# Preparing the fifth attention half three units later, and the second network's weight conversion nine units later, in a fused attention and two-network kernel

## The chip, the core and the metric

The kernel runs on one core of one Trainium2 chip. The metric is the device time of one execution in microseconds (us), as the median of several runs; lower is better. The core's engines are named as in the profile: PE (TensorE, matmuls), PEld (TensorE's weight loads), DVE (VectorE), ACT (ScalarE), POOL (GpSimd) and SP (SyncE, which here issues nearly all transfers).

## The reference

Three stages run one after the other. The first is a linear attention with a decaying state: 4 batches, 8 heads, 768 steps, head size 48. Its output, 3072 tokens of 384 numbers, goes through a network with a rational activation (384 to 2048 to 384), and then through a second network with a softmax-weighted activation and a normalisation (384 to 1024 to 384).

```
state = alpha[:, :, t, :, None] * state + einsum('bhd,bhe->bhde', k[:, :, t], v[:, :, t])
y[:, :, t] = einsum('bhd,bhde->bhe', q[:, :, t], state)
...
h = x @ w_in
P = a[0] + a[1]*h + a[2]*h**2 + a[3]*h**3
Q = 1.0 + abs(b[0])*abs(h) + abs(b[1])*h**2
x2 = (P / (Q + 1e-06)) @ w_out
...
h = x2 @ w_in2
solu = h * softmax(h)
out = (normalise(solu) * g_ln) @ w_out2
```

## The kernel before

**Chunks and units.** The 768 steps are cut into 6 chunks of 128 steps; with 4 batches a chunk has 512 tokens. The first network runs over one chunk after the other. A **unit** is one chunk and one block of 128 of the 2048 hidden columns, so a chunk has 16 units (`NF1`), and there are 96 (`NU`), counted by `u`. For each unit `m_up` multiplies (9 matmuls of 128x512, line 595, into the PSUM tile `hp`), ACT, DVE and POOL compute the rational activation, and `m_down` of the unit four before (`LAG = 4`) multiplies again (9 matmuls, line 641, into `x2p`). Numbers are split into a high and a low part, which is why each product takes three matmuls. Units below 24 with an even number (`MIX`) give part of the activation to POOL: DVE has three passes there, lines 613, 618 and 619; the other units have four, lines 621, 624, 625 and 626. `hp` has three buffers: the matmuls of unit u wait for the last DVE pass (line 619 or 626) of unit u-3.

**Halves.** A chunk's attention is done in two **halves** of two batches each, so there are 12, counted by `i` from 0. From `i = 2` on, a half is **prepared** by `a_dve`: transposes of alpha, k and q (lines 291 and 296), a running product (scan `P`, line 309), a reverse scan (line 318), a product (line 321), two transposes back (line 325), with POOL's product at line 336, which SP then moves through DRAM into the tiles `qks` (lines 338 and 277) and `kns` (lines 330 and 283). **Computed** it is by `a_pe`: two rounds of scores on PE (`sc`, line 421), copied by ACT (line 428) and masked by POOL (line 429), then the outputs `y` (line 445), written to the next chunk's input `xt` (lines 471 and 472), and the state update `u` (lines 486, 496 and 497).

**Order around the change.** The main loop over `u` calls `half_steps(i)` at every eighth unit, when `u` modulo 8 is `LATE = 2`: half 2 at unit 2, half 3 at unit 10, half 4 (the fifth) at unit 18, and so on. It makes one step of `a_pe(i)` and two steps of the preparation of half `i + 1` in each unit. So the fifth half is prepared in units 10 to 14, beside the computation of half 3. The helper `pin` ties those steps to work of units shortly before; within that the order on each engine is settled by the scheduler when the program is built, and is then fixed: each engine works its list in order.

**Weights.** The inputs of both networks' weights are 64-bit numbers; `split_w` brings them in (line 536), converts them on DVE (lines 540, 543 and 544), and splits them on ACT and POOL (lines 550 and 551). The first network's are converted in groups during the first chunk. The second network's are converted by `w2_split`, 14 steps (six of 512 columns, eight of 384), and stored to DRAM (line 553). One step is taken in each unit from `U2 = 15` on in which `IDLE` holds: units 15, 16, 24, 25, 32, 33 and so on to 64, 65. They are read again from unit 80 on.

Of the kernel before, what the change touches and what calls it, by code (L numbers as in the profile page):

```python
# [23 lines left out]
def _run(*gens):  # L24
    for g in gens:
        for _ in g:
            pass
# [3 lines left out]
def kernel(  # L31
# [25 lines left out]
    NF1 = DF1 // 128  # L57
# [5 lines left out]
    NPE = 2  # L63
# [12 lines left out]
    GS = 2  # L76
# [4 lines left out]
    SKIP = (5, 7, 11)  # L81
    AHEAD = 3
    HOLD = (1, NCH - 1)
    LATE = 2
    U2, IDLE = NF1 - 1, lambda u: (u + (u < NF1 + 4)) % (NF1 // 2) < 2
    assert (B, H, D, CH) == (4, 8, 48, 128)

    const = ctx.enter_context(tc.tile_pool(name="const", bufs=1, side="left"))
# [65 lines left out]
    def network(fast):  # L154
# [98 lines left out]
        def a_load(i, names=("ra", "rk", "rq")):  # L253
            for x, (src, nm) in enumerate(((alpha, "ra"), (k, "rk"), (q, "rq"))):
                if nm not in names:
                    continue
                if i == 1:
                    t = borrow(3, 2048 + 1024 * x, [16 * D + 16])
                elif i == 0 and nm == "rq":
                    t = borrow(3, 5120, [16 * D + 16])  # L260
                else:
                    t = ap_.tile([128, 16 * D + 16], F32, name=nm, tag="rk" if nm == "rk" else "ra")
                if i < NPE:
                    nc.gpsimd.memset(t[:, 16 * D:], 1.0)
                for y in range(B):
                    c, b, h = slot(i, y)
                    nc.sync.dma_start(  # L267
                        out=t[32 * y:32 * y + 32, :16 * D].rearrange("p (h x) -> p h x", h=4),
                        in_=src[b, h:h + 4, CH * c:CH * c + CH, :].rearrange("h (j r) d -> j h (r d)", r=4),
                    )  # L270
                raws[i, nm] = t
                yield

        def a_move_qk(i):
            qk, kb = moved[i]
            for m, i0, n, d0 in ((0, 0, 32, 0), (1, 0, 16, 32), (1, 16, 16, 64), (2, 0, 32, 80)):
                nc.sync.dma_start(out=qks[d0:d0 + n], in_=qk[m].rearrange("b i x -> i b x")[i0:i0 + n])
            yield
# [122 lines left out]
        def a_prep(i):  # L401
            if i >= NPE:
                yield from a_dve(i)

        def a_enter(i):
            if i < NPE:
                v_load(i)
                yield from a_turn(i)
            else:
                yield from a_move(i)  # L410

        def a_pe(i):
# [21 lines left out]
            end = ap_.tile([128, B, 2], F32, name="end", tag="end", bufs=2)  # L434
# [38 lines left out]
            yield  # L473
            if i >= NPE:
                yield
            if i >= 2 * NPE:
                yield
            if i < NPE:
                a_back(i)
            u = ps_ap.tile([128, B * 2, D], F32, name="u", tag="at")  # L480
# [185 lines left out]
        def w2_load(nm):  # L666
            src = {"i": w2i_d, "o": w2o_d}[nm]
            n, step = {"i": (KT, 1), "o": (NF2, 4)}[nm]
            for z in range(0, n, step):
                for x, y in enumerate("hl"):  # L670
                    nc.sync.dma_start(out=w2[nm + y][:, z:z + step].bitcast(F32), in_=src[:, x, z:z + step])
                    yield
# [140 lines left out]
        def chain(*gens):  # L813
            for g in gens:
                yield from g
# [34 lines left out]
        now = [0]  # L850
        NU = NCH * NF1
# [4 lines left out]
        def pin(n):  # L856
            stack = ExitStack()
            if n <= now[0] < NU and fast:
                for e, u in (("PE", now[0]), ("ACT", now[0] - n), ("POOL", now[0] - n)):
                    stack.enter_context(tc.issue_after(last[e, u].ins))  # L860
                stack.enter_context(tc.issue_after(fin[now[0] - n].ins))
            return stack

        def half_steps(i):
            gp = a_pe(i)
            gd = chain(a_prep(i + 1), a_move_qk(i + 1) if i + 1 >= NPE else iter(()), a_load(i + 2, ("ra", "rk")) if i + 2 < NH and i + 1 >= NPE else iter(())) if i + 1 < NH else iter(())
            while True:
                with pin(GP):
                    a = next(gp, "end")
                with pin(GS):  # L870
                    b = next(gd, "end")
                    if b != "end":
                        b = next(gd, "end")
                if a == "end" and b == "end":
                    if i + 1 < NH:
                        _run(a_enter(i + 1))
                        if i + 2 < NH and i + 1 < NPE:
                            _run(a_load(i + 2))
                    return
                yield  # L880
# [6 lines left out]
        for u in range(NU + LAG):  # L887
            c, f = divmod(u, NF1)
            now[0] = u
            if f % (NF1 // 2) == LATE and u < NU:  # L890
                _run(side)
                i = 2 * c + 2 + f // (NF1 // 2)
                side = half_steps(i) if fast and i < NH else iter(())
            if u < NU:
                if f == 0 and c == NCH - 1:
                    if fast:
                        judge(moe_pool)
                    open2()
                    tail = chain(w2_load("i"), n_load(0), w2_load("o"))
                if f == 0 and c and not fast:  # L900
                    x_load(c)
                if fast and u < NF1:
                    if f % 4 == 0:
                        _run(prep)
                        if f:
                            stage["near"] = False
                            stage["bank"] = ""
                        prep = w1_group(f // 4 + 2) if f < 8 else iter(())
                    with later(G1):
                        take(prep, 1)  # L910
                m_up(u)
                if fast and u < NF1:
                    with later(G1):
                        take(prep, 1)
            if u == NU:
                _run(n_load(1))
            take(side, 1)
            if u >= U2 and IDLE(u):
                stage["bank"] = "at"
                with later(G2):  # L920
                    take(split2, 1)
            if tail is not None:
                _run(split2)
                take(tail, 2)
            if u >= LAG:
                held.append(u - LAG)
            if not (f == LAG and HOLD[0] < c < HOLD[1]):
                while held:
                    m_down(held.pop(0))
            if u - NU + NF1 in EARLY:  # L930
                n_tile(EARLY.index(u - NU + NF1))
                if len(EARLY) == B and u - NU + NF1 == EARLY[-1]:
                    n_turn(0)
        ps_h.__exit__(None, None, None)
        ps_x2.__exit__(None, None, None)
        end = ExitStack()
# [106 lines left out]
    with tc.If(wide > 0):  # L1043
        recurrence()
        network(False)
# [30 lines left out]
```

## Time and profile before

| | us |
|---|---|
| median of 3 runs | 771.57 |
| lowest and highest | 770.66, 771.99 |
| the profiled execution | 771.29 |
| its span, first to last instruction | 769.4 |
| busy in the span: PE | 727.3 |
| DVE | 625.1 |
| ACT | 535.2 |
| POOL | 359.2 |

The profiled execution's time is 1.89 us above its span. Busy times are sums over the whole span; the stages have different limits, so the stretches around units 10 to 20 have to be read by themselves. In the trace unit 10's first matmuls start at 120.44 us and unit 20's at 177.09 us.

### The profile page before, as it was taken

How to read it: one execution, taken by the hardware profiler on the slowest of the kernel's cores; microseconds unless marked ns; L12 is line 12 of the kernel's file. 1: busy time of each engine (PE TensorE's matmuls, PEld its weight loads, DVE VectorE, ACT ScalarE, POOL GpSimd, SP SyncE). 2: the span in 40 equal slices, each digit the busy share in tenths (PEclk: the TensorE clock that was granted, in tenths of full speed). 3: DMA queues.
4: the chain of work that ended last, by engine and by line, in shares of the span. 5: the costliest groups of instructions: out<-in, count | busy, mean ns of one | idle time of the engine just before them, and what ended most of it. 6: DMA issues, size and time to landing. Idle time of an engine off the chain costs nothing.

```text
span 769.4 us, 13908 instructions
## 1 busy us (share of the span) xinstructions
PE 727.3 (95%) x4976; PEld 605.7 (79%) x4976; DVE 625.1 (81%) x1111; ACT 535.2 (70%) x984; POOL 359.2 (47%) x306
## 2 busy tenths in 40 slices
PE   4686999999999999999999999999999999999996
PEld 3575767788888888778787788888888989988996
DVE  5999999989899989898998966567787797877630
ACT  2245867688878878797979788888965565555641
POOL 3255787877555345444445523422243333442322
PEclk9857899999999999999999999999999999999998
DMA  7994447475747483726554350820025354451552
GB/s 174 264 278 153 106 149 173 127 171 174 165 153 182 136 182 95 186 79 193 133 146 89 117 91 1 302 109 0 2 83 126 96 123 117 114 123 43 138 130 67
DMA packets 87278, 101.74 MB, mean 132 GB/s; under 512 B 34464, under 2 KB 63136, under 8 KB 87200
## 3 DMA queue, kind: packets, MB, share of 16 engines
q1 hardware_dynamic: 87008, 100.41, 49.2%
q8 instruction: 41, 0.67, 0.4%
q10 hardware_dynamic: 192, 0.36, 0.2%
q14 instruction: 37, 0.30, 0.1%
HBM read 60.59 MB, written 27.56 MB: 115 GB/s over the span
## 4 chain that ended last, share of the span: by engine, by line
PE 58%; DVE 24%; issue 5%; DMA 5%; ACT 4%; SPq 2%; POOL 0%; DVEq 0%; ACTq 0%; POOLq 0%
PE hp L595 14%; PE x2p L641 13%; PE op L787 13%; PE h L716 13%; DVE w L624 3%; DVE hp L625 2%; DVE p L626 2%; DVE p L621 2%; SPq L267 2%; PE y L445 2%; DMA rq<-in_q_dram 1%; DVE qk L291 1%; DVE ft L544 1%; DVE alT L325 1%; DVE fp L543 1%
## 5 line engine op out<-in xcount | busy, mean ns | idle before, releaser
L595 PE MATMUL hp<-xt,g 128*128 128x512 f32 x864 | 222.8, 401 | 15.6 <-DVE p L619 7.5
L629 POOL TENSOR_TENSOR gl<-p,gh 128x512 fp32r<-128x512 f32 x96 | 134.6, 1402 | 206.0 <-ACT gh L628 117.7
L595 PEld LDWEIGHTS hp<-xt,g 128*128 128x128 f32 x864 | 163.1, 192 | 57.3 <-DVE p L626 11.2
L641 PE MATMUL x2p<-gh,g 128*128 128x512 f32 x576 | 195.5, 395 | 0.4 <-ACT gh L628 0.4
L641 PEld LDWEIGHTS x2p<-gh,g 128*128 128x128 f32 x576 | 107.7, 188 | 26.3 <-ACT gh L628 1.6
L641 PE MATMUL x2p<-gl,g 128*128 128x512 f32 x288 | 113.0, 392 | 0.0
L787 PE MATMUL op<-w2oh,room 128*128 128x384 f32 x384 | 101.5, 338 | 0.0
L779 POOL TENSOR_TENSOR room<-room,room 128x1024 fp32r<-128x1024 f32 x22 | 53.8, 2448 | 101.7 <-ACT room L778 81.0
L624 DVE SCALAR_TENSOR_TENSOR w<-w,co,hp 128x512 f32<-128x512 f32 x84 | 62.0, 738 | 45.4 <-ACT hp L623 44.5
L716 PE MATMUL h<-w2ih,x 128*128 128x512 f32 x288 | 90.8, 394 | 0.0
L602 ACT ACTIVATE p<-hp,co 128x512 f32<-128x512 f32 x96 | 66.1, 688 | 13.7 <-POOL gl L629 13.0
L603 ACT ACTIVATE w<-ah,co 128x512 f32<-128x512 f32 x96 | 69.4, 724 | 6.9 <-DVE hp L625 6.7
L787 PEld LDWEIGHTS op<-w2oh,room 128*128 128x128 f32 x384 | 70.1, 188 | 0.9
L600 ACT ACTIVATE ah<-hp 128x512 f32<-128x512 f32 x96 | 57.0, 593 | 16.2 <-PE hp L595 15.6
L621 DVE SCALAR_TENSOR_TENSOR p<-p,co,hp 128x512 f32<-128x512 f32 x84 | 61.8, 736 | 7.6 <-ACT p L602 7.3
L623 ACT ACTIVATE hp<-ah 128x512 f32<-128x512 f32 x84 | 50.2, 598 | 25.3 <-DVE p L621 24.3
L787 PE MATMUL op<-w2ol,room 128*128 128x384 f32 x192 | 65.0, 339 | 0.0
L628 ACT ACTIVATE gh<-p 128x512 fp32r<-128x512 f32 x96 | 59.9, 624 | 6.6 <-PE x2p L641 3.4
L641 PEld LDWEIGHTS x2p<-gl,g 128*128 128x128 f32 x288 | 54.1, 188 | 11.7 <-issue 0.8
L626 DVE SCALAR_TENSOR_TENSOR p<-p,co,hp 128x512 f32<-128x512 f32 x84 | 62.4, 742 | 1.0
L716 PEld LDWEIGHTS h<-w2ih,x 128*128 128x128 f32 x288 | 53.9, 188 | 11.7
L622 ACT ACTIVATE ah<-w,co 128x512 f32<-128x512 f32 x84 | 60.8, 724 | 1.1
(168 smaller groups left out, 1258.6 us busy)
## 6 DMA issues: line engine op xcount, KB each, us to landing
room<-room SPq DMA_DIRECT2D x94, 128.0 KB, 2.4
qk_d<-qk SPq DMA_DIRECT2D x10, 771.0 KB, 4.1
st<-in_moe_w_in_dram SPq DMA_DIRECT2D x13, 512.0 KB, 4.6
st<-in_moe_w_out_dram SPq DMA_DIRECT2D x16, 384.0 KB, 3.2
qks<-qk_d SPq DMA_DIRECT2D x20, 257.0 KB, 4.3
x<-x_d SPq DMA_DIRECT2D x18, 256.0 KB, 3.1
out_dram<-o SPq DMA_DIRECT2D x94, 48.0 KB, 1.6
ra<-in_alpha_dram SPq DMA_DIRECT2D x44, 96.0 KB, 2.4
```

What stands on the lines that cost most here:

```text
L595: last["PE", u] = nc.tensor.matmul(hp, lhsT=w[:, kt, 128 * o:128 * o + 128], rhs=xts[c][:, kt, xx, :], start=(kt == 0 and w is hi and xx = ...
L602: nc.scalar.activation(p, hp, AF.Square, bias=co[:, 7:8])
L603: nc.scalar.activation(w, ah, AF.Square, bias=co[:, 6:7])
L621: nc.vector.scalar_tensor_tensor(p, p, a1, hp, ALU.add, ALU.mult)
L622: nc.scalar.activation(ah, w, AF.Ln, bias=rest)
L624: nc.vector.scalar_tensor_tensor(w, w, rest, hp, ALU.add, ALU.mult)
L626: fin[u] = nc.vector.scalar_tensor_tensor(p, p, a0, hp, ALU.add, ALU.mult)
L628: last["ACT", u] = nc.scalar.activation(gh, p, AF.Copy)
L629: last["POOL", u] = nc.gpsimd.tensor_tensor(gl, p, gh[:].bitcast(F32), ALU.subtract)
L641: nc.tensor.matmul(x2ps[c][d], lhsT=w[:, o, 128 * d:128 * d + 128], rhs=gg, start=(f == 0 and w is hi and gg is gh), stop=(f == NF1 - 1 an ...
L716: nc.tensor.matmul(hp[:, 512 * n:512 * n + 512], lhsT=x2s[c][:, kt, x, CH * b:CH * b + CH], rhs=w2[w][:, kt, 512 * n:512 * n + 512], start ...
L787: nc.tensor.matmul(op, lhsT=x[:, 128 * f:128 * f + 128], rhs=w2[w][:, f, :], start=(f == 0 and x is hi and w == "oh"), stop=(f == NF2 - 1 ...
```

## The change

Three edits to when things are issued; no computation is added or taken away.

- The preparation of the fifth half (issued beside half 3) begins at unit 13 instead of 10, by `WAIT = {3: 13}`. At two steps a unit it now takes units 13 to 17.
- `half_steps(4)`, with the fifth half's scores and the preparation of the sixth, begins at unit 19 instead of 18. One empty step of `a_pe` is left out for this half, so its state update stays at unit 23 and the halves after it stay where they were.
- `w2_split` begins at unit 24 instead of 15: units 24, 25, 32, 33 and so on to 72, 73.

```
-    LATE = 2
-    U2, IDLE = NF1 - 1, lambda u: (u + (u < NF1 + 4)) % (NF1 // 2) < 2
+    LATE = lambda u: u % (NF1 // 2) == (3 if u // (NF1 // 2) == 2 else 2)
+    WAIT = {3: 13}
+    U2, IDLE = NF1 + 4, lambda u: u % (NF1 // 2) < 2
...
-            if i >= 2 * NPE:
+            if i > 2 * NPE:
                 yield
...
-                with pin(GS):
-                    b = next(gd, "end")
-                    if b != "end":
+                b = None
+                if now[0] >= WAIT.get(i, 0):
+                    with pin(GS):
                         b = next(gd, "end")
+                        if b != "end":
+                            b = next(gd, "end")
...
-            if f % (NF1 // 2) == LATE and u < NU:
+            if LATE(u) and u < NU:
```

Line numbers of the functions above are one higher in the changed kernel. The lists of the engines are the same in both kernels up to unit 9's first DVE pass; there they part.

On DVE, between unit 9's first pass (line 621) and its last (line 626), the list before holds the fifth half's transposes of alpha and its scan:

```order
L543 SCALAR_TENSOR_TENSOR ft<-st,ft 128x384
L296 STREAM_TRANSPOSE alT<-ra 128x4x32
L624 SCALAR_TENSOR_TENSOR w<-w,co,hp 128x512
L544 SCALAR_TENSOR_TENSOR ft<-st,ft 128x384
L309 SCALAR_TENSOR_TENSOR P<-alT,d_109 128x774
L613 SCALAR_TENSOR_TENSOR hp<-p,co,hp 128x512
L540 TENSOR_SCALAR ft<-st 128x384
L625 SCALAR_TENSOR_TENSOR hp<-w,hp 128x512
L496 TENSOR_TENSOR Sbd<-Sbd,u 48x8x48 x2
L618 SCALAR_TENSOR_TENSOR hp<-hp,co,ah 128x512
L543 SCALAR_TENSOR_TENSOR ft<-st,ft 128x384
L626 SCALAR_TENSOR_TENSOR p<-p,co,hp 128x512
```

and of the change the same stretch, up to unit 9's last pass (now line 627):

```order
L544 SCALAR_TENSOR_TENSOR ft<-st,ft 128x384
L545 SCALAR_TENSOR_TENSOR ft<-st,ft 128x384
L625 SCALAR_TENSOR_TENSOR w<-w,co,hp 128x512
L614 SCALAR_TENSOR_TENSOR hp<-p,co,hp 128x512
L541 TENSOR_SCALAR ft<-st 128x384
L626 SCALAR_TENSOR_TENSOR hp<-w,hp 128x512
L497 TENSOR_TENSOR Sbd<-Sbd,u 48x8x48 x2
L544 SCALAR_TENSOR_TENSOR ft<-st,ft 128x384
L541 TENSOR_SCALAR ft<-st 128x384
L627 SCALAR_TENSOR_TENSOR p<-p,co,hp 128x512
```

The transposes and the scan are gone from it, and one more conversion piece of the first network's weights (a second line 541) stands ahead of the last pass.

Still on DVE, from unit 13's last pass to the state update of half 3 (`Sbd`), the list before holds the first two conversion steps of the second network's weights (`fp`):

```order
L626 SCALAR_TENSOR_TENSOR p<-p,co,hp 128x512
L472 TENSOR_TENSOR xt<-y,xt 128x2x256
L472 TENSOR_TENSOR xt<-y,xt 128x256
L540 TENSOR_SCALAR fp<-st 128x512
L543 SCALAR_TENSOR_TENSOR fp<-st,fp 128x512
L613 SCALAR_TENSOR_TENSOR hp<-p,co,hp 128x512
L544 SCALAR_TENSOR_TENSOR ft<-st,fp 128x512
L540 TENSOR_SCALAR fp<-st 128x512
L543 SCALAR_TENSOR_TENSOR fp<-st,fp 128x512
L618 SCALAR_TENSOR_TENSOR hp<-hp,co,ah 128x512
L544 SCALAR_TENSOR_TENSOR ft<-st,fp 128x512
L496 TENSOR_TENSOR Sbd<-Sbd,u 48x8x48 x2
```

and of the change, with the second part of the fifth half's preparation there:

```order
L627 SCALAR_TENSOR_TENSOR p<-p,co,hp 128x512
L292 STREAM_TRANSPOSE qk<-rq 128x2x4x32
L614 SCALAR_TENSOR_TENSOR hp<-p,co,hp 128x512
L326 STREAM_TRANSPOSE alT<-qk 128x3x4x32 x2
L297 STREAM_TRANSPOSE qk<-rq 128x4x32 x2
L619 SCALAR_TENSOR_TENSOR hp<-hp,co,ah 128x512
L292 STREAM_TRANSPOSE qk<-rq 128x2x4x32
L620 SCALAR_TENSOR_TENSOR p<-w,hp 128x512
L622 SCALAR_TENSOR_TENSOR p<-p,co,hp 128x512
L497 TENSOR_TENSOR Sbd<-Sbd,u 48x8x48 x2
```

The conversion has left this place. The preparation's first part now stands between unit 11's last pass and unit 13's last.

On SP, before, the transfers of the fifth half stand behind two loads of the second network's weights (line 536), and two stores of them (line 553) stand behind:

```order
L536 DMA st<-in_moe_w_in_dram 128x512 x2
L330 DMA kb_d<-alT 128x768
L267 DMA ra<-in_alpha_dram 32x4x192 x4
L338 DMA qk_d<-qk 128x3x514
L277 DMA qks<-qk_d 32x4x514
L277 DMA qks<-qk_d 16x4x514 x2
L277 DMA qks<-qk_d 32x4x514
L349 DMA vns<-in_v_dram 128x8x48 x2
L283 DMA kns<-kb_d 128x4x192
L553 DMA w2i_d<-st 256x1x512 x2
```

and of the change:

```order
L331 DMA kb_d<-alT 128x768
L350 DMA vns<-in_v_dram 128x8x48
L268 DMA ra<-in_alpha_dram 32x4x192 x4
L350 DMA vns<-in_v_dram 128x8x48
L284 DMA kns<-kb_d 128x4x192
L339 DMA qk_d<-qk 128x3x514
L278 DMA qks<-qk_d 32x4x514
L278 DMA qks<-qk_d 16x4x514 x2
L278 DMA qks<-qk_d 32x4x514
```

The loads and stores of weights have left, and `vns` and `kns` now stand ahead of the move of `qks`.

## Rows read from the trace of the kernel before

**Rows 1.** Windows by engine: length, then busy us (instructions), clock, DMA share, GB/s.

```profile
118.00:151.00 33.00, 30.46 (x266) 24.08 (x264) 32.77 (x56) 23.27 (x43) 26.40 (x23) 1.00 0.57 147
151.00:300.00 149.00, 149.00 (x1135) 121.30 (x1134) 135.53 (x222) 127.17 (x230) 83.27 (x76) 1.00 0.63 161
440.00:480.00 40.00, 40.00 (x322) 32.63 (x321) 27.09 (x40) 33.75 (x60) 14.13 (x14) 1.00 0.30 60
```

**Rows 2.** Timeline of PE, 130 to 150 us: start, length, instruction, idle before.

```profile
131.77 2.16 PE L421 MATMUL sc<-qks 48*128 48x128 f32 x16
135.16 2.34 PE L595 MATMUL hp<-xt,g 128*128 128x512 f32 x9 [1.23 <-DVE p L626]
...
142.15 0.41 PE L445 MATMUL y<-A,vns 128*32 128x128 f32 x4 [0.74 <-POOL A L429]
...
148.00 0.73 PE L595 MATMUL hp<-xt,g 128*128 128x512 f32 x2 [0.57 <-DVE p L626]
```

**Rows 3.** Windows on DVE, instructions of tile alT alone: length, busy (instructions).

```profile
123.80:134.30 10.50, 3.66 (x5) 1.00 0.75 180
134.30:147.20 12.90, 4.66 (x4) 1.00 0.39 121
```

**Rows 4.** The same of tile qk alone, the whole preparation.

```profile
123.80:149.20 25.40, 6.47 (x13) 0.38 (x2) 0.00 (x0) 1.00 0.55 151
```

**Rows 5.** Groups of DVE, 123.8 to 149.2 us, by shape: busy, mean ns, idle before.

```profile
L325 DVE STREAM_TRANSPOSE alT<-qk 128x384 f32<-128x384 f32 x2 | 1.6, 855 | 0.0
...
L321 DVE TENSOR_TENSOR qk<-qk,alT 128x768 f32<-128x768 f32 x1 | 0.9, 945 | 0.0
```

**Rows 6.** Timeline of DVE: last passes of units 9, 11 and 14.

```profile
134.37 0.73 DVE L626 SCALAR_TENSOR_TENSOR p<-p,co,hp 128x512 f32<-128x512 f32 x1
...
147.24 0.71 DVE L626 SCALAR_TENSOR_TENSOR p<-p,co,hp 128x512 f32<-128x512 f32 x1
...
160.78 0.68 DVE L619 SCALAR_TENSOR_TENSOR p<-w,hp 128x512 f32<-128x512 f32 x1
```

**Rows 7.** Timeline of POOL: state products, two masks of scores, the preparation's product.

```profile
134.01 2.03 POOL L497 TENSOR_TENSOR Sbd<-Sbd,end 48x384 f32<-48x384 f32 x2
...
139.99 2.10 POOL L429 TENSOR_SCALAR_AFFINE_SELECT A<-A 128x512 f32<-128x512 f32 x1
...
146.92 0.64 POOL L429 TENSOR_SCALAR_AFFINE_SELECT A<-A 128x512 f32<-128x512 f32 x1
...
149.26 1.74 POOL L336 TENSOR_TENSOR qk<-qk,P 128x768 f32<-128x768 f32 x1 [0.44 <-DVE qk L291]
```

**Rows 8.** Groups of DVE, 153 to 159.1 us: the second network's first two conversions.

```profile
L543 DVE SCALAR_TENSOR_TENSOR fp<-st,fp 128x512 int32<-128x512 int32 x2 | 1.4, 698 | 0.1
L540 DVE TENSOR_SCALAR fp<-st 128x512 int32<-128x512 int32 x2 | 1.4, 696 | 0.1
L544 DVE SCALAR_TENSOR_TENSOR ft<-st,fp 128x512 int32<-128x512 int32 x2 | 1.4, 680 | 0.0
```

**Rows 9.** Timeline of PE around units 17 to 19.

```profile
164.21 4.24 PE L595 MATMUL hp<-xt,g 128*128 128x512 f32 x18
...
169.75 1.16 PE L421 MATMUL sc<-qks 48*128 48x128 f32 x16
...
173.01 2.20 PE L595 MATMUL hp<-xt,g 128*128 128x512 f32 x9
```

**Rows 10.** Timeline of SP's queue: the move of the fifth half's qks.

```profile
152.46 0.39 SPq L338 DMA_DIRECT2D qk_d<-qk  x1
156.56 1.73 SPq L277 DMA_DIRECT2D qks<-qk_d  x4
```

**Rows 11.** Transfers of tile qks, 140 to 240 us: time from issue to landing.

```profile
DMA to landing us min/median/max: 3.3/4.4/5.7
```

**Rows 12.** Timeline of PE: idle behind the conversions of units 48 and 56.

```profile
328.91 2.34 PE L595 MATMUL hp<-xt,g 128*128 128x512 f32 x9 [0.26 <-DVE p L626]
...
366.67 0.98 PE L641 MATMUL x2p<-gh,g 128*128 128x512 f32 x3 [0.37 <-ACT gh L628]
```

## The prediction

> **What bounds the kernel now.** I read the busy time by stretches first, because the share over the whole span mixes stages. From 118 to 151 us, which is units 10 to 14, DVE is busy 32.77 of 33.00 us and PE 30.46; from 151 to 300 us it is the other way round, PE 149.00 of 149.00 and DVE 135.53 [rows 1]. So DVE sets the pace up to unit 14 and PE sets it afterwards, and the change takes work out of the first stretch and puts it into the second. Busy PE time says nothing about who holds PE up, so the timeline of PE comes next: behind 118 us PE waits three times, 1.23 us at unit 12 and 0.57 us at unit 14 for DVE's last pass of the unit three before (line 626), and 0.74 us for a mask made by POOL [rows 2]. That is 2.54 us, and the difference 33.00 - 30.46 says the same. In the whole list of waits of PE there is none between 151 and 300 us. PE's work from there on is one row without holes, so whatever PE gains before 151 us reaches the end, and no more than about 2.54 us can be gained there by removing waits.
>
> **What leaves units 10 to 14.** The fifth half's preparation on DVE is 8.32 us in instructions that touch alT (3.66 + 4.66, nine of them) [rows 3] and 6.47 us in those that touch qk (thirteen) [rows 4]; lines 321 and 325 touch both and count once, 0.9 + 1.6 = 2.5 us [rows 5]. Together 8.32 + 6.47 - 2.5 = 12.3 us of DVE. ACT's checks and POOL's product (line 336) go with it, and of SP's transfers kb_d, qk_d, qks, and the loads that wait for the transposes.
>
> Unit 12's matmuls wait for unit 9's last pass. On DVE 3.66 us of the preparation stand between unit 9's first pass and its last at 134.37 [rows 3, 6]. Without them the last pass starts near 134.37 - 3.66 = 130.7, and the conversion piece that the new order puts ahead of it (at most 0.7 us [rows 8]) makes it 131.4, its end 132.1. PE has its earlier work done at 131.77 + 2.16 = 133.9 [rows 2]. The 1.23 us go, with 1.8 us to spare. Unit 14 waits for unit 11's last pass, at 147.24 [rows 6]; all of the preparation but its last transpose stands ahead of it, so it could come more than 11 us earlier. It is then held by its own inputs instead, but PE wants it only at 148.00 - 0.57 - 0.74 - 1.23 = 145.5: the 0.57 us go.
>
> The 0.74 us are less sure, since POOL makes the mask. That mask took 2.10 us where another took 0.64, and 2.03 us of the state update (line 497) had gone ahead of it in POOL's list [rows 7]. In the new order line 497 comes earlier, but two conversion pieces and two activation products still stand ahead of the third mask. Between nothing and all of it, I take 0.7 us, because the slow mask alone is 1.46 us longer than the short one and the ACT copy it follows is no longer behind DVE. Sum: 1.23 + 0.57 + 0.70 = 2.5 us gained by unit 15.
>
> **What enters units 13 to 17.** The 12.3 us come back behind unit 11's last pass, and the first two conversions of the second network's weights, 1.4 + 1.4 + 1.4 = 4.2 us of DVE [rows 8], leave the same place. Up to unit 14's last pass (160.78 to 161.4 [rows 6]) DVE therefore has the same work as before less 4.2 us, and would be through at 157.2 if it did not idle. Unit 17's matmuls need that pass. They started at 164.21 [rows 9] without a wait; with 2.5 us gained and three matmuls now placed behind them (0.7 us, as eighteen took 4.24 [rows 9]) PE asks for it near 161. So 3.8 us of idling by DVE are covered, and I cost the move at nothing. If that cover were gone, unit 17 would wait by the excess, once, and the units behind it would follow with the same delay.
>
> **The scores at unit 19.** They need qks, whose move is queued on SP behind kns and the loads of alpha. Before, SP issued qk_d at 152.46, the four transfers of qks from 156.56 for 1.73 us, and these land 4.4 us later [rows 10, 11]: 162.7, for scores at 169.75 [rows 9]. Now the last transpose ends near 157 and POOL's product (1.74 us [rows 7]) near 159; adding 4.1, 1.7 and 4.4 gives 169.2. PE reaches the scores behind unit 19's matmuls. Those ended at 173.01 + 2.20 = 175.2, with a score round of 1.16 us and three more matmuls (0.7 us) ahead of them than now [rows 9]; less these and 2.5 us that is 170.8. The margin is 1.6 us, where it was 7. It holds by this reckoning, and costs nothing. The half's output is needed at unit 32 only, and its state update stays at unit 23, so the later score round by itself delays nobody.
>
> **The conversions at the other end.** They stop at units 72 and 73 instead of 64 and 65. Units 15 and 16 cost PE nothing before. The pairs at units 48 and 56 cost it 0.26 and 0.37 us [rows 12]; from 440 to 480 us, where the new pair falls, DVE is busy 27.09 of 40.00 us [rows 1], so a pair should cost between nothing and 0.37: I take 0.3. Of the pair at units 40 and 41 the columns become 512 instead of 384; such pairs at 24 to 33 cost PE nothing, so nothing here. Nothing of the second network's own order on PE, ACT and DVE changes.
>
> **Sum.** 771.29 - 2.5 + 0.3 = 769.1 for the profiled execution. The median of the runs is 0.28 us higher, so I forecast 769.4.
>
> **One rule against the sum.** PE's busy time hides waits inside the pipelined matmuls, if there are any. The weight loads show it: 24.08 us in 33.00 against 121.30 in 149.00 [rows 1], so at the later density 24.08 x 149.00 / 121.30 = 29.6 us would do, and 3.4 us could go. But the scores of half 3 take 2.16 us per sixteen where the interleaved ones take 1.16 [rows 2, 9], thirty-two of them, and their order on PE stays; that explains 2 of the 3.4. The Trainium skill, page "Perfetto Trace Analysis", section "Identifying the Most-Contended Engine", says that matmul busy share is a bad measure and that weight-load busy share is a good one. By it the gain would be 3.4 us, by the row of waits 2.5; the trace bears the rule out only as far as the scores' order leaves something.
>
> **The rivals.**
>
> *The waits change their owner.* DVE is no longer late, but ACT and POOL are in the chain of each unit: unit 11's last pass needs ACT's two steps behind unit 8's product on POOL, and DVE idles there. For it: POOL was busy 26.40 of 33.00 us in the stretch and ACT 23.27 [rows 1], and the conversion pieces of the first network's weights are crowded together now. Then only the wait at unit 12 goes: 1.23 - 0.3 = 0.9 us, 770.7. If DVE's work merely meets PE three units later, the gain is returned there, and the change does nothing: 771.6.
>
> *The scores at unit 19 wait for qks.* This one ends slower. If DVE works units 13 to 15 first and the preparation idles behind ACT, its last transpose may end a unit and a half late, 7 us; qks lands at 176, PE waits 176.2 - 170.8 = 5.4 us and the sum becomes 771.57 - 2.2 + 5.4 = 774.8. It decides from 2.2 + 1.6 = 3.8 us of lateness on: below, some of the gain is left. Against it: the margin of 1.6 us adds to DVE's 3.8 us of cover.
>
> *More than the waits goes.* PE gains what its weight loads show, 3.4 us, and the last pair costs nothing: 768.2.
>
> **How the numbers follow.** A difference of 0.2%, 1.5 us, is about what a measurement of this kernel can tell from no change; the forecast is 2.2 us. Chances: the forecast 0.55, the waits that change owner or come back 0.27, more than the waits 0.08, the late scores 0.10. The forecast's case reaches from 768.6 (all 2.54 us, no cost at the end, and 0.4 us of run spread) to 770.2 (no gain from POOL's mask, a cost of 0.37), so a small part of it, 0.03, lies within 0.2%. Faster: 0.52 + 0.08 + 0.02 of the first rival = 0.62; same: 0.25 + 0.03 = 0.28; slower 0.10. The range of 8 in 10 leaves out the late scores and the lower end of the last rival: 768.0 to 771.7.
>
> **What the profile of the changed kernel would show.** Right: no PE wait for line 627 at units 12 and 14, unit 15's first matmuls near 151.5 instead of 154.08, unit 17's near 161, no wait ahead of the scores at unit 19, DVE no longer full from 124 to 140 us, and a PE wait under 0.4 us near units 72 and 73. Wrong would be: a PE wait for a POOL product or an ACT copy in units 12 to 14, a wait of units 16 to 18 for line 620 or 627, qks landing behind unit 19's matmuls, or a PE row whose holes between 300 and 450 us grow by over a microsecond because the conversions meet other work there.

## The result, and the profile after

The changed kernel is slower: 775.76 us (median of 22 runs) against 771.04 (22 runs of the kernel before beside them), a ratio of 1.0056 with the interval 1.0041 to 1.0072. Half a per cent is little, but the interval leaves out 1. The profiled execution took 774.82 us, its span is 773.1, 3.7 more than before. Lines of the changed kernel are one higher.

The stretches that answer to [rows 1] (columns as there):

```profile
118.00:151.00 33.00, 30.16 (x250) 23.84 (x251) 28.75 (x44) 22.35 (x40) 22.51 (x22) 0.90 0.36 76
151.00:300.00 149.00, 146.48 (x1125) 119.39 (x1116) 138.54 (x223) 122.55 (x221) 77.17 (x72) 1.00 0.62 164
```

DVE was relieved in the first stretch, 28.75 us where it had 32.77. PE gained nothing by it: it idles 33.00 - 30.16 = 2.84 us where it idled 2.54. And in the second stretch it now idles 2.5 us where it idled none. The waits of PE that answer to [rows 2] and [rows 9], and one near the end that has no counterpart before:

```profile
130.61 1.68 PE L422 MATMUL sc<-qks 48*128 48x128 f32 x16 [0.92 <-PE x2p L642]
134.22 4.21 PE L596 MATMUL hp<-xt,g 128*128 128x512 f32 x9 [1.92 <-DVE p L627]
...
176.08 0.46 PE L422 MATMUL sc<-qks 48*128 48x128 f32 x2 [0.88 <-DMA qks<-qk_d]
...
178.17 1.13 PE L422 MATMUL sc<-qks 48*128 48x128 f32 x14 [1.63 <-DMA qks<-qk_d]
...
749.20 0.45 PE L788 MATMUL op<-w2oh,room 128*128 128x384 f32 x1 [0.58 <-ACT room L779]
```

The waits of unit 14 and for POOL's mask are gone in this execution, but unit 12's wait for unit 9's last pass is longer, PE waits 0.92 us ahead of the scores before it, and the scores at unit 19 wait for `qks`, 0.88 + 1.63 = 2.51 us. The row at 134.22 shows another loss: its nine matmuls took 4.21 us, where before nine took 2.34. The clock that the chip granted to PE shows why (windows, columns as in [rows 1]; the clock is the third number from the end):

```profile
130.00:134.00 4.00, 1.68 (x16) 1.52 (x16) 3.94 (x4) 1.80 (x4) 3.84 (x4) 0.82 0.95 175
134.00:138.00 4.00, 3.78 (x9) 3.01 (x10) 3.77 (x7) 2.45 (x5) 2.83 (x4) 0.50 0.00 0
138.00:142.00 4.00, 4.00 (x15) 2.99 (x14) 2.84 (x5) 3.97 (x8) 2.88 (x4) 0.82 0.00 0
```

Behind PE's idle 0.92 and 1.92 us the granted clock is 0.50, the lower of its two levels (1.2 of 2.4 GHz), and then rises again.

Reading the starts of the same unit in both traces, the changed kernel is 1.47 us early at unit 10 (in work that both have in the same order, so this is chance), 3.96 late at unit 28, 2.77 late at the end of the first network, and 3.7 late at the end. So about 1 us of this execution's loss arises in the second network, of which the prediction had said that nothing changes there, and 2.8 us in the first, 4.2 if one counts from unit 10. The page shows it as well, in the chain that ended last, by engine. Of before:

```profile
PE 58%; DVE 24%; issue 5%; DMA 5%; ACT 4%; SPq 2%; POOL 0%; DVEq 0%; ACTq 0%; POOLq 0%
```

and of after:

```profile
DVE 41%; PE 26%; ACT 10%; issue 8%; DMA 8%; SPq 5%; POOL 1%; ACTq 0%; DVEq 0%; POOLq 0%
```

Before, the end hangs on PE's row; after, it hangs on DVE's chain of small steps in the second network (maximum, exponential, normalisation, transpose), which PE has caught up with near 750 us.

### The profile page after: what moved, and what is told of

Same layout as the page of the kernel before. It is cut to its first block, busy times and chain, and to the rows that moved or that the text cites. A ratio compares the mean times of both kernels' runs of the same rounds, so it can differ in the third digit from the quotient of the medians.

```text
span 773.1 us, 13904 instructions
## 1 busy us (share of the span) xinstructions
PE 730.6 (95%) x4976; PEld 608.5 (79%) x4976; DVE 630.7 (82%) x1111; ACT 535.8 (69%) x984; POOL 355.8 (46%) x306
## 4 chain that ended last, share of the span: by engine, by line
DVE 41%; PE 26%; ACT 10%; issue 8%; DMA 8%; SPq 5%; POOL 1%; ACTq 0%; DVEq 0%; POOLq 0%
PE hp L596 10%; PE x2p L642 9%; DVE room L757 3%; DVE room L740 3%; DVE w L625 3%; ACT jk L742 2%; SPq L769 2%; DVE hp L626 2%; PE op L788 2%; DVE sm L736 2%; SPq L268 2%; DVE qk L292 2%; DVE p L622 2%; DMA room<-room 2%; DVE p L627 2%
```

## Where the second network loses: a code fetch among the transfers

The second network turns each tile of 128 tokens by a DVE transpose and sixteen transfers for four tiles (tile `room`, line 768, in the changed kernel 769). Beside them the trace has 41 transfers of 16 KB on the queue named q8 with the kind "instruction". PE has by far the longest list (4,976 matmuls and as many weight loads), and the fetches come about 25 us apart there, so they are taken to be PE's code; no row says whose they are. In the kernel before, the sixteen transfers start at 619.99 us and a fetch starts 4.5 us later. The queues in the window 624.4 to 624.6 us (packets, MB, share of the engines):

```profile
q8 instruction: 1, 0.02, 40.1%
```

In the changed kernel they start at 622.80, and the fetch starts 2.0 us later. Window 624.7 to 624.9 us:

```profile
q8 instruction: 1, 0.02, 31.4%
```

The transfers that are on their way then land later. The first four, which bring the first tile, before (619.9 to 622.5 us, five issues):

```profile
DMA to landing us min/median/max: 2.2/2.3/2.4
```

and after (622.7 to 625.3 us, four issues):

```profile
DMA to landing us min/median/max: 2.3/3.3/3.5
```

Before, the fetch delays the sixth to eighth transfer (they land 3.5 to 3.8 us behind their issue). These belong to the second tile, and ACT's copy of it waits for them:

```profile
627.96 1.06 ACT L778 ACTIVATE room<-room 128x1024 fp32r<-128x1024 f32 x1 [1.19 <-DMA room<-room]
```

That keeps POOL's products for the first and the second tile apart. After, the fetch delays the second to fourth, ACT's copy of the first tile starts 5.16 instead of 4.30 us behind the first issue, the second tile comes undelayed behind it, and the two products of POOL run back to back. Timeline of DVE and POOL before:

```profile
625.43 2.40 POOL L779 TENSOR_TENSOR room<-room,room 128x1024 fp32r<-128x1024 f32 x1 [17.69 <-ACT room L778]
625.71 2.14 DVE L751 TENSOR_TENSOR sm<-sm 128x1 f32<-128x1 f32 x1 [0.81 <-ACT sm L750]
...
628.08 0.16 DVE L753 SCALAR_TENSOR_TENSOR sm<-sm 128x1 f32<-128x1 f32 x1
628.27 0.81 DVE L754 TENSOR_SCALAR room<-room,sm 128x1024 f32<-128x1024 f32 x1
```

and after:

```profile
629.10 4.90 POOL L780 TENSOR_TENSOR room<-room,room 128x1024 fp32r<-128x1024 f32 x2 [18.56 <-ACT room L779]
629.38 2.15 DVE L752 TENSOR_TENSOR sm<-sm 128x1 f32<-128x1 f32 x1 [1.68 <-ACT sm L751]
631.56 0.16 DVE L753 SCALAR_TENSOR_TENSOR sm<-sm 128x1 f32<-128x1 f32 x1
631.75 2.26 DVE L754 SCALAR_TENSOR_TENSOR sm<-sm 128x1 f32<-128x1 f32 x1
634.05 0.81 DVE L755 TENSOR_SCALAR room<-room,sm 128x1024 f32<-128x1024 f32 x1
```

An instruction on 128x1 numbers, 0.16 us when alone, takes 2.15 us and ends with POOL's product; the next but one takes 2.26 us and ends with POOL's second. Before, 1.26 us lie between the two products, and the second step passes in 0.16. So DVE reaches its 128x1024 step (line 754, now 755) 5.78 us later than before, 3.0 us more than PE is late. Of the 5.78 us, 4.64 are left at the transpose near 660 us; from then on the chain mostly repeats every 7.40 us per tile, and its last transpose is still 4.33 us later than before, PE only 2.77.

The Trainium skill, page "SBUF — State Buffer", section "SBUF: two separate sides", says that VectorE and GpSimd share one port pair under an exclusive lock, and that the one that comes second is blocked for the whole instruction, a VectorE operation with two inputs in SBUF among them. These rows agree: the held steps end within 0.02 us of POOL's product.

What moves the fetch? Counted in the traces, PE's list holds 8610 instructions up to the wait that PE passes 3.3 us behind the first of the sixteen transfers in the kernel before, and 8614 in the changed kernel: four more semaphore waits, since PE's order around units 10 to 20 is another. This was the theory for the later experiments: **four instructions more on PE shift a code fetch, and the fetch costs the second network one to four microseconds.** The rival: all of the loss lies in the first network, in the waits at units 12 and 19.

The list's length alone does not place the fetch, though. Counted by the instructions that PE had started, the fetch behind this one starts at 8858 to 8865 in all fourteen profiles of this document, whatever the kernel; this one starts at 8600 to 8606 where it is early and at 8619 to 8626 where it is late, which is a step of more than four. What decides between the two places is not shown.

## The experiments

In each table row the ratio is to runs of the kernel before that were taken beside it (medians of before 771.18 for e1 to e4, 770.68 for e5 to e8, 770.42 for e9 to e12; 29 to 35 runs). The ratio is not the quotient of the two medians (e11: 769.65 / 770.42 = 0.999, against 0.997), so a difference below can come out otherwise by the ratios than by the medians. "PE's list" is the number of its instructions up to the wait named above, and the last column is read from the one profiled execution, in us.

| kernel | us | runs | ratio, interval | PE's list | fetch behind the first transfer |
|---|---|---|---|---|---|
| changed | 775.76 | 22 | 1.0056, 1.0041 to 1.0072 | 8614 | 2.0 |
| e1_w2only | 769.79 | 12 | 0.9991, 0.997 to 1.0012 | 8610 | 4.5 |
| e2_preponly | 777.47 | 6 | 1.0078, 1.0048 to 1.0109 | 8615 | 2.0 |
| e3_scores20 | 777.43 | 12 | 1.0063, 1.0039 to 1.0088 | 8613 | 2.6 |
| e4_prep11 | 774.44 | 12 | 1.0027, 1.0002 to 1.0053 | 8614 | 1.9 |
| e5_before_pad2 | 773.88 | 12 | 1.0038, 1.0017 to 1.006 | 8614 | 2.6 |
| e6_before_pad2_late | 771.18 | 12 | 0.9999, 0.9975 to 1.0024 | 8610 | 2.6 |
| e7_after_drop2 | 772.67 | 12 | 1.003, 1.0003 to 1.0057 | 8610 | 5.2 |
| e8_prep11_drop2 | 771.13 | 12 | 1.0001, 0.9976 to 1.0027 | 8610 | 5.1 |
| e9_after_fast4 | 771.39 | 14 | 1.0009, 0.999 to 1.0028 | 8614 | 2.6 |
| e10_before_fast4 | 769.93 | 12 | 0.9989, 0.9971 to 1.0007 | 8610 | 5.2 |
| e11_w2only_fast4 | 769.65 | 12 | 0.997, 0.9948 to 0.9992 | 8610 | 5.1 |
| e12_scores20_drop2 | 772.27 | 12 | 1.0013, 0.9992 to 1.0033 | 8609 | 6.0 |

The first four look for the loss in the first network.

**e1_w2only** is the kernel before with the third edit alone:

```
-    U2, IDLE = NF1 - 1, lambda u: (u + (u < NF1 + 4)) % (NF1 // 2) < 2
+    U2, IDLE = NF1 + 4, lambda u: u % (NF1 // 2) < 2
```

> Only the third edit: the second network's weights converted from unit 24, the fifth half prepared and scored as before. Theory A (the loss is the scores of unit 19 waiting for qks, 2.5 us in the changed kernel's profile, and the wait at unit 12 with the half clock behind it): neither is touched, so no loss, 0 to -1 us, qks lands long before the scores. Theory B (the conversions' new places cost the time, in units 72 and 73 or by their transfers): slower by about 4 us, as the whole change.

Measured 0.9991: the later conversion costs nothing that can be measured. The loss is in the other two edits.

**e2_preponly** is the changed kernel with that line put back.

> The first two edits without the third: the fifth half prepared from unit 13 and scored at unit 19, the weights converted in units 15 and 16 as before. Theory A: the two conversions (4.2 us of VectorE, two stores on SP between the moves) push the preparation's end later still, so the wait of the scores for qks grows from 2.5 us to between 3 and 8; slower than before by 5 to 9 us, so worse than the whole change. Theory B: the loss is gone, within 1 us of before.

Measured 1.0078. The preparation and the scores alone carry the whole loss. But PE waits 0.21 + 0.95 us for `qks` in its profile, less than in the changed kernel and not the 3 to 8 us expected.

**e3_scores20** is the changed kernel with the fifth half's scores one unit later again:

```
-    LATE = lambda u: u % (NF1 // 2) == (3 if u // (NF1 // 2) == 2 else 2)
+    LATE = lambda u: u % (NF1 // 2) == (4 if u // (NF1 // 2) == 2 else 2)
...
-            if i >= NPE:
+            if i >= NPE and i != 2 * NPE:
```

> The changed kernel with the fifth half's scores at unit 20 instead of 19 (a second empty step left out, so the state update stays at unit 23). TensorE comes to the scores some 4 us later, which is more than the 2.5 us that qks was late. Theory A: no wait for qks, so 2 to 2.5 us faster than the changed kernel, 1 to 2.5 us slower than before. Theory B, or if the wait for qks was covered elsewhere anyway: as slow as the changed kernel, 4 us.

PE waits for `qks` nowhere in its profile, and the time is 777.43, no better than the changed kernel. So taking away the wait for `qks` alone did not help. Near the end its profile shows a wait that is as long (PE):

```profile
750.90 0.45 PE L788 MATMUL op<-w2oh,room 128*128 128x384 f32 x1 [2.99 <-ACT room L779]
```

**e4_prep11** starts the preparation at unit 11 (`WAIT = {3: 11}`).

> The changed kernel with the fifth half prepared from unit 11 instead of 13. qks lands about 8 us earlier than in the changed kernel, ahead of unit 19. Theory A: no wait for qks; the loss left is that of unit 12 alone, so between -1 and +2 us against before. Theory B: 4 us slower, since the conversions stand where the change put them.

Here too the wait for `qks` is gone, PE is 0.90 us ahead of the kernel before at the end of the first network, and yet the time is 1.0027. The same wait near the end eats the gain:

```profile
747.75 0.66 PE L788 MATMUL op<-w2oh,room 128*128 128x384 f32 x1 [2.81 <-ACT room L779]
```

What e2, e3, e4 and the changed kernel have in common, against the kernel before and e1, is the place of the fetch. The next four test that.

**e5_before_pad2** adds two small matmuls to the kernel before, at the start of the second network's first tile; the next matmul overwrites their result. The orders of DVE, ACT, POOL and SP stay as they were; on PE some neighbours between 493 and 518 us (units 81 to 86) change places.

```
+            [nc.tensor.matmul(hp[:, :64], lhsT=x2s[c][:, 0, 0, CH * b:CH * b + CH], rhs=w2["ih"][:, 0, :64], start=True, stop=True) for z in range(2 if s == 0 else 0)]
```

> The kernel before, with two more matmuls of 128x64 (results overwritten by the next one) at the start of the second network's first tile, near 500 us. Theory of the code fetch: what all four slower kernels share in the second network is that one 16 KB instruction fetch (queue q8) starts about 2 us behind the first of sixteen transposed transfers (tile room, near 620 us), where it starts 4.5 us behind it in the kernel before, because PE's list holds 3 to 5 more instructions ahead of it. Two more matmuls are four more instructions, so this kernel shows the fetch near 2 us, the first tile's copy on ACT 0.85 us later, two POOL products back to back with DVE held beside them, and a PE wait for tile room near 750 us: 772.5 to 776. Rival, all the loss lies in the first network: two small matmuls cost 0.1 us, 771.1 to 771.4, and no PE wait near 750 us.

Measured 773.88, ratio 1.0038, as the fetch theory had it and not the rival. The fetch lies 2.6 us behind the first transfer, and POOL and PE read:

```profile
625.56 4.90 POOL L779 TENSOR_TENSOR room<-room,room 128x1024 fp32r<-128x1024 f32 x2 [18.97 <-ACT room L778]
```

```profile
745.61 0.45 PE L787 MATMUL op<-w2oh,room 128*128 128x384 f32 x1 [0.89 <-ACT room L778]
```

**e6_before_pad2_late** has the same pair at tile 14 (`s == 14`).

> The same two extra matmuls, but at the start of tile 14 of the second network, behind 640 us, so behind the fetch in question. Theory of the code fetch: the fetch near 624 us stays 4.5 us behind the first transposed transfer; 770.5 to 771.8. Rival (two more matmuls or their order cost by themselves): the same time as the kernel with the early pair.

Measured 0.9999: two more matmuls by themselves cost nothing that can be measured. But its profiled execution (771.76 us) shows the fetch at 2.6 us, and with it the two held steps and a PE wait of 0.84 us near 745 us, which the theory had not expected: with 8610 instructions ahead, the place is not the same in every execution. Seven other profiles with 8609 or 8610 instructions have it at 4.5 to 6.0 us, all six with 8613 to 8615 at 1.9 to 2.6. So the link from the list to the fetch rests on one profile for each kernel, and what e5 and e6 show by their runs is that two matmuls ahead of the fetch cost time and two behind it do not.

The step from the fetch to the loss is the same wherever it was seen. In the six profiles with the early fetch and tile 4 still on POOL (changed, e2 to e6) a first step of DVE is held for 2.13 to 2.15 us and the next but one for 2.26 to 2.32; in the five with the late fetch (before, e1, e7, e8, e12) only the first is. From the end of the first network's last matmul to the end of the span, the six take 187.65 to 192.08 us, the five 186.39 to 187.49.

**e7_after_drop2** is the changed kernel without two matmuls of unit 95, and **e8_prep11_drop2** is e4 with the same edit:

```
-                for w, gg in ((hi, gh), (hi, gl), (lo, gh)):
+                for w, gg in ((hi, gh), (hi, gl), (lo, gh))[:2 if u == 95 and d < 2 else 3]:
...
-                        start=(f == 0 and w is hi and gg is gh), stop=(f == NF1 - 1 and w is lo),
+                        start=(f == 0 and w is hi and gg is gh), stop=(f == NF1 - 1 and (w is lo or gg is gl and u == 95 and d < 2)),
```

> The changed kernel, with two matmuls left out of the last unit of the first network (unit 95: the low part of w_out for two of its three column blocks, so these outputs lack a small correction). That is four instructions fewer ahead of the fetch, as in the kernel before, and 0.47 us less of PE. Theory of the code fetch: the fetch goes back to 4.5 us behind the first transposed transfer, no PE wait near 750 us, and the time falls by 0.47 and by 1.2 or more: 772 to 774.1, the rest of the loss being in the first network. Rival, all in the first network: 775.3.

> The changed kernel with the preparation from unit 11 (774.4, its profile 0.9 us ahead of the kernel before at the end of the first network), with the same two matmuls of unit 95 left out. Theory of the code fetch: no PE wait for tile room near 750 us, 769 to 770.5, faster than the kernel before. Rival: 774.0, only the two matmuls' 0.47 us gone.

Measured 772.67 and 771.13, in each 3.1 to 3.3 us below the kernel that it comes from, by the ratios 2.0 us (0.26% of 771) in both, of which 0.47 is the work left out. The fetch is back at 5.2 and 5.1 us, and neither has a PE wait near 750 us. The edit also makes a few neighbours on PE, DVE and ACT change places between 590 and 607 us, and in e7 one DVE step near 170 us; what this does by itself was not measured. e7 met its expectation; e8 came down too, but to the time of the kernel before and not below it.

**e12_scores20_drop2** does the same to e3.

> The changed kernel with the fifth half's scores at unit 20 (777.4 by itself, no PE wait for qks), with the two matmuls of unit 95 left out as before (the low part of w_out for two of its column blocks). Theory of the code fetch: the fetch goes back behind the first tile's transfers, the PE wait of 2.99 us near 750 us goes, and the time falls by 4.5 to 5.5 us: 772 to 773. Rival, the loss of the later scores lies in the first network: 776.9.

Measured 772.27, 5.2 us below e3 (by the ratios 3.9), as expected; the PE wait near 750 us is gone. In these three pairs the two kernels were not measured beside each other, but each against the kernel before.

**e9_after_fast4**, **e10_before_fast4** and **e11_w2only_fast4** leave the fetch where it is and take away what it does: tile 4's low part goes from POOL to DVE, so that one POOL product less stands beside DVE.

```
-    FASTS = (0, 20)
+    FASTS = (0, 4, 20)
```

> The changed kernel, with the low part of the second network's tile 4 taken by DVE instead of POOL, so that one POOL product less runs beside DVE near 630 us. Theory of the held DVE: in the changed kernel two POOL products back to back (4.90 us) hold two of DVE's smallest instructions for 2.15 and 2.26 us, and that, more than the copy's 0.85 us, makes the transposes late; with one product gone the delay of the last transpose shrinks by about 2 us and the PE wait near 750 us with it: 773 to 774.7. Rival: the late landing alone does it, and DVE, which now takes tile 4's low part itself, waits for it in its own list: 775.5 or more.

> The kernel before with tile 4's low part on DVE. Theory of the held DVE: the fetch lies behind the first tile's transfers here in most executions, and one hold of 2.14 us becomes 1.3 us of DVE's own work: 770 to 771, and fewer slow executions. Rival: DVE's list waits for the copy, 771.5 to 773.

> The kernel before with only the later conversion of the second network's weights (769.8 by itself), and tile 4's low part on DVE: the version that should beat both kernels if the held DVE costs in some executions: 768.5 to 769.8. Rival: 770.5 to 772.

e9: 771.39, 4.4 us below the changed kernel and better than expected. Its fetch is still 2.6 us behind the first transfer and its copy still late (5.15 us); DVE's small steps pass, and one larger step is held (2.50 us instead of 0.81), beside the product of tile 5:

```profile
630.13 1.23 DVE L780 TENSOR_TENSOR room<-room,room 128x1024 fp32r<-128x1024 f32 x1 [1.34 <-ACT room L779]
631.27 0.15 DVE L752 TENSOR_TENSOR sm<-sm 128x1 f32<-128x1 f32 x1
...
633.14 2.50 DVE L755 TENSOR_SCALAR room<-room,sm 128x1024 f32<-128x1024 f32 x1
```

PE has no wait near 750 us there, and the second network takes 186.49 us from the first network's last matmul, against 187.65 in the changed kernel and 186.75 before. So it is the holding of DVE, more than the late landing, that makes the chain late. The profiled execution is the slowest of e9's fourteen, 774.82 us, and stands for its median only in the second network: its loss lies in the first, where the granted clock was 0.50 from 131.8 to 138.6 us, behind the wait at unit 12, and from 176.1 to 183.0, behind the wait for `qks`, and where PE is 3.94 us late at the end. The edit does little to the kernel before: e10 is at 769.93, and its twelve runs span 768.81 to 771.41, where the 35 of the kernel before beside them span 768.68 to 776.87. That the kernel before pays a little of the hold in some executions would fit, but four of its 35 runs lie above 774 us, and twelve runs can miss such by chance. e11, the later conversion with this edit, has the lowest ratio: 769.65, 0.997 (0.9948 to 0.9992), clear of the kernel before but not of e1 or e10.

## Why the prediction was wrong, point by point

**"Whatever PE gains before 151 us reaches the end."** This step failed in e4, which is 0.90 us ahead at the end of the first network and 3.6 behind at the end of the span. A PE row without holes says that nothing has made PE wait yet; it does not say how close the next chain is. In the kernel before, ACT and DVE make the high and the low part of tile 20, the last chunk's first tile, in two halves each:

```profile
743.52 1.16 ACT L778 ACTIVATE room<-room 128x512 fp32r<-128x512 f32 x2 [1.40 <-DMA room<-room]
744.19 1.29 DVE L779 TENSOR_TENSOR room<-room,room 128x512 fp32r<-128x512 f32 x2 [5.09 <-ACT room L778]
```

The first half of the high part is ready at 744.16 us, and PE starts the tile at 745.68: 1.5 us of slack, in a stretch that I called PE's. In the changed kernel that half is ready 5.0 us later, at 749.14, and PE would have come 2.9 later, at 748.62: so it waits. What remained unread was the second network's chain on DVE and ACT. A gain of PE in the first network does get through where nothing delays this chain: in e1's profile PE is 2.98 us early at the end of the first network and 2.23 at the end.

**"Nothing of the second network's own order on PE, ACT and DVE changes."** True, and not enough: its transfers met a code fetch at another place. By the four pairs that move the fetch (before and e5, changed and e7, e4 and e8, e3 and e12) this costs 0.38%, 0.26%, 0.26% and 0.5%; less the 0.47 us left out in three of them, 1.5 to 3.4 us. No rival of mine had it.

**"The 1.23 us go, with 1.8 us to spare."** Wrong in both terms. I reckoned unit 9's last pass at 131.4; it started at 133.41:

```profile
130.54 1.93 DVE L544 SCALAR_TENSOR_TENSOR ft<-st,ft 128x384 int32<-128x384 int32 x1
132.40 0.98 DVE L541 TENSOR_SCALAR ft<-st 128x384 int32<-128x384 int32 x1
133.41 0.75 DVE L627 SCALAR_TENSOR_TENSOR p<-p,co,hp 128x512 f32<-128x512 f32 x1
```

The two conversion pieces in front of it took 1.93 and 0.98 us, where I gave 0.7 to the one; POOL was busy 3.84 of 4.00 us beside them (the clock's rows above). Whether POOL held them up is not shown: unlike the steps near 630 us they do not end with a POOL instruction. And PE came to unit 12 at 132.29 and not at 133.9, mostly because this execution was 1.47 us early. In e7, whose clock stayed at 1.00 there, 1.09 us of the 1.23 remain and 0.74 for POOL's mask again, and in e8 PE's waits from unit 10 to 28 sum to 2.33 us, before to 2.54:

```profile
133.22 2.33 PE L596 MATMUL hp<-xt,g 128*128 128x512 f32 x9 [1.06 <-DVE alT L304]
...
144.75 0.50 PE L642 MATMUL x2p<-gl,g 128*128 128x512 f32 x1 [0.38 <-POOL gl L630]
...
148.30 0.75 PE L446 MATMUL y<-A,vns 128*32 128x128 f32 x17 [0.89 <-POOL A L430]
```

That is the rival "the waits change their owner", in its form without any gain: with less DVE work, PE waits for another engine there. e8, with neither the wait for `qks` nor the early fetch, and with 0.47 us of work less, is at 1.0001. The forecast's gain of 2.5 us was in no kernel that moves the preparation.

**"The margin is 1.6 us" (scores at unit 19).** This is the term that the forecast put at nothing and that cost most in the first network. It was wrong by more than 8 us in the landing: `qks` was there at 178.0, not at 169.2. SP's queue, answering to [rows 10]:

```profile
161.03 2.79 SPq L268 DMA_DIRECT2D ra<-in_alpha_dram  x4
163.92 0.39 SPq L350 DMA_DIRECT2D vns<-in_v_dram  x1
164.41 0.53 SPq L284 DMA_DIRECT2D kns<-kb_d  x1
164.98 0.51 SPq L339 DMA_DIRECT2D qk_d<-qk  x1
...
171.14 1.74 SPq L278 DMA_DIRECT2D qks<-qk_d  x4
```

I had let the preparation end at 157 as if DVE only had to work; its last transposes ended near 161, POOL's product started at 162.2, `qk_d` was issued at 164.98 and took 6.1 us to land where I gave 4.1, and `qks` 5.6 where I gave 4.4. The rival "the scores at unit 19 wait for qks" named this place. Its price is 2.51 us of waiting in this profile. Two pairs that differ in the start of the preparation alone (changed and e4, e7 and e8) put it at 1.3 and 1.5 us by the medians, 2.2 us (0.29%) by the ratios, with overlapping intervals; in e7's profile the granted clock falls to 0.50 from 175.9 to 179.3 us behind this wait, which is part of the price. The rival gave the right side, but the wait is less than half of its 5.4 us, and its time of 774.8 lay near the result by luck, through losses that it did not have.

**The conversions.** The 0.3 us for units 72 and 73 did no harm; e1 and e11 show the third edit at -0.1% and, both with tile 4 on DVE, -0.2% against e10, neither of which can be told from nothing.

**The sum as measured.** The forecast's 2.2 us of gain became a loss of 0.56%, 4.3 us, by the ratios. With the second network's part covered in both (e9 and e10) the three edits cost 0.2%, 1.5 us (the intervals overlap), in place of the gain; the rest of the 0.56%, 2.8 us, would then be the second network. By e7, where the fetch is late, the first network costs more, 0.3% and the 0.47 us of work left out, 2.8 us together, and the second 1.5. So both parts are there, and how the loss is shared between them is known no better than that.

**The weight loads.** Those in the first stretch are 23.84 us, 24.08 before: the density that the forecast's last rival counted on did not rise, and its gain of 3.4 us did not appear; PE still waits there (2.84 us). That gain was worked out by the rule on weight-load share (the Trainium skill, page "Perfetto Trace Analysis", section "Identifying the Most-Contended Engine"), which tells how far PE is from its peak and not how much of that a change takes.

**Its own signs.** Of the signs of being wrong that the prediction named, one came: `qks` landed behind unit 19's matmuls. Of the signs of being right, the wait under 0.4 us near units 72 and 73 held (there is none); that no wait is left at unit 12, that unit 15 starts near 151.5 us (it was 154.70) and unit 17 near 161 (164.16) did not.

What stays open: why the fetch came early in e6's profiled execution, and so whether the longest runs of the kernel before (774 to 777) are those with an early fetch. Open too is the clock's share. The loss by the lower clock near 134 us, 4.21 - 2.34 = 1.9 us for these nine matmuls, differs between executions: the kernel before has it near 110 us instead (0.85 over units 8 and 9, 11.12 us where the changed kernel took 9.57). But it is not chance alone. Over its 22 runs the changed kernel's granted clock has the mean 0.967, over the 99 runs of the kernel before that have one on record 0.970; the five slowest of the 22 (777.62 to 779.32 us) are at 0.964 to 0.966, the four fastest (771.37 to 772.16) at 0.967 to 0.972. A difference of 0.003 over 773 us would take up to 2.3 us from PE (an estimate, as if PE always had work). From 125 to 760 us the low stretches of all profiles lie at or just behind waits of PE, near 134 and 176 us and, in e3 and e4, near 750 us (0.50 from 752.8 to 756.2 and from 747.8 to 751.2), so the lower clock is read here as a part of what those waits cost; how large a part, no run shows.

## What to carry to other kernels

Before a wait is taken away, read how much slack the next chain has at the far end, not only whether the engine's row has holes: here PE had 1.5 us of slack near 745 us, and a chain that came 2 us later against PE made it wait. When a change moves the time although the rows around it barely move, compare the start of the same unit all along both traces; a good part of the loss was 600 us behind the edit. And where a transfer that much depends on shares its engines with code fetches, make the consumer robust (a product less on POOL beside DVE's small steps) instead of hoping for the fetch's place.

## What the runs showed of the hardware

- Beside a 16 KB instruction fetch the three transfers that were on their way took 3.2 to 3.5 us to land instead of 2.3, and SP's issue 1.47 us instead of 0.59.
- Counted by PE's started instructions, one of these fetches started at either of two places in fourteen profiles, 8600 to 8606 or 8619 to 8626, and the one behind it always at 8858 to 8865.
- Two extra matmuls of 128x64, in a list of some 10,000 instructions, made a kernel of 771 us slower by 2.9 us (0.38%, interval 0.17 to 0.60); the same two behind the fetch did not (0.9999).
- Instructions of DVE on 128x1 numbers took 2.15 us instead of 0.16 beside a POOL product on SBUF, and ended with it, while a DVE transpose (1.25 us) and reduction (1.20 us) beside such a product kept their length.
- The granted clock fell to 0.50 behind PE's idle 0.92 and 1.92 us near 132 us in the changed kernel's profile and stayed at 1.00 behind idle 0.88 and 1.63 near 177; in e7's, with the same list up to there, it stayed at 1.00 behind idle 1.09 at 132 us and fell behind idle 1.09 and 1.56 near 174.
